# A hand-written order of 634 pieces of a fused retention and channel-mix kernel: its last 264 pieces in another order

## The chip, the cores and the metric

The kernel runs on one core of a Trainium2 chip. The metric is the device time of one execution in microseconds (us), taken on the chip; smaller is better. One further execution was recorded by the hardware profiler; the views of the profile come from that one.

## What is computed

The first half is a recurrent retention layer: 4 batches, 8 heads, 768 tokens, head width 64, with a decay `gamma` for each head. The second half is a channel mix on its output of width 512: two mixes of each token with the token before, a square-of-relu layer of width 1024, and a sigmoid gate.

```
state = gamma * state + k_t (outer) v_t           # for each head
y_t   = q_t . state / 8
x     = y, heads side by side                     # 4 x 768 x 512
xk    = mu_k * x + (1 - mu_k) * x_prev;  xr the same with mu_r
k     = relu(xk @ w_k);  v = (k * k) @ w_v
out   = sigmoid(xr @ w_r) * v
```

All inputs and the output are float32.

## The kernel before, in words

The 3072 tokens are cut into 12 blocks of 256 (n = 0 to 11, three to a batch). Everything is written out in one string, ORDER, as about 634 pieces. A piece is a code, the block, sometimes more numbers, the PSUM banks that it writes after an @, and the engine after a ~ (v VectorE/DVE, a ScalarE/ACT, p GpSimd/POOL, s SyncE/SP; no letter is TensorE/PE). The loop at the end of the kernel walks the string once and emits the instructions of each piece, so **the string is the program order of every engine's queue**; semaphores between the engines follow from the data. No other planner acts on it at run time. Each engine takes its own pieces strictly in the order of the string, and waits where a piece's data or buffer isn't ready.

The pieces that matter here, with the line of the instruction as the profile gives it:

- `lq`, `lk`, `lv` (L229, L234): loads of q, k, v of a block. `Tq`, `Tk` (L271, L277): transposes on PE, 32 small matmuls each for blocks 6 to 11; `Eq`, `Ek` (L240, ACT) copy them out of PSUM.
- `S` (L317, 32 matmuls) scores, `M` (L346, DVE) their mask; `vs` (L252, DVE) scales v; `C` (L365) the new state, `U` (L418, DVE) adds the old one in four steps, `G` decays it (L427 as one DVE instruction, L423 as four ACT instructions). `I` (L440) and `Y` (L461 and L440) make the retention's output in PSUM, `D` (L506, DVE, two instructions) scales it into x.
- `dx` (L528, DVE) is x minus x_prev; `X` (L557, DVE) mixes it, w = 0 for xk and w = 1 for xr, in four slices j. Blocks 3 and 4, 6 and 7, 9 and 10 share these.
- `K` (L571 for shared blocks, four matmuls of 512 columns; L581 for single ones, eight of 256): xk @ w_k. `Qa` (L590, ACT) relu, `Qb` (L598, L602, ACT) square. `R` (L611, four of 512): the gate's matmul; `s` (L617, ACT) its sigmoid.
- `V` (L623): (k*k) @ w_v for half a block of tokens, in two halves of four matmuls of 512 columns; `O` (L629, DVE) multiplies with the gate and frees the PSUM bank; `st` (L636, SP) stores 256 KB. For the last half block `Vc` (L641, eight of 256 columns), `Oc` (L648) and `sc` (L656) do this in two column halves.
- `z` are matmuls on zeros at the start, `cm` (L678, DVE) makes the masks, `mt` and `me` turn the mu vectors.

Two kinds of buffers tie the queues together. PSUM has eight banks: a PE piece that begins a bank waits until the last reader of that bank (an ACT or DVE piece) is through. And rings in SBUF: the output tiles OS are a ring of four, numbered 2n + tb, so `O.8.1` (17) writes the tile that `st.6.1` (13) has to have stored, and the gate tiles RS are a ring of four as well.

PE alternates between full matmuls (128 x 128 weights: K, R, V, Vc) and small ones (64 x 64 tiles: T, S, C, I, Y). A stretch of small pieces in a row is called a small run below.

Of the kernel before, what the change touches and what calls it, by code (L numbers as in the profile page):

```python
# [29 lines left out]
S.1.1@23 M.1.1~v C.1@01 U.1.0~v z.2@4 I.1@23 S.1.0@67 X.0.0.1~v t.0.1.2~a X.0.0.2~v Tk.2@0 t.0.1.3~a  # L30
t.0.0.0~a M.1.0~v X.0.0.0~v z.2@4 Y.1 t.0.1.1~a X.0.0.3~v Ek.2~a K.0.0@0 K.0.1@6 lq.4~p U.1.1~v
G.1~a wr~p lk.4~p D.1~v dx.1~v X.1.0.2~v X.1.0.0~v K.0.2@1 Qa.0.0~a Qb.0.0~a Qa.0.2~a lq.3~p
X.1.0.1~v X.1.0.3~v X.1.1.0~v Qa.0.1~a K.0.3@0 Qa.0.3~a lk.3~p vs.2~v Tq.2@1 X.1.1.2~v K.1.3@6
K.1.0@0 C.2@7 U.2.0~v lv.3~p Eq.2~a S.2.1@23 M.2.1~v S.2.0@45 M.2.0~v Qb.0.3~a lv.4~p K.1.1@1
X.1.1.1~v Qa.1.0~a t.0.1.0~a K.1.2@7 I.2@23 Qb.0.1~a Qa.1.1~a wv.0~p Qb.0.2~a Tq.4@01 Eq.4~a Y.2
Qa.1.3~a Qb.1.1~a X.0.1.3~v X.1.1.3~v R.1.1@4 Tk.4@01 Ek.4~a J.2 R.1.0@6 Qa.1.2~a s.1.0~a X.0.1.2~v
X.0.1.1~v X.0.1.0~v R.0.1@5 s.0.1~a s.1.1~a R.0.0@7 s.0.0~a S.4.1@01 Qb.1.0~a D.2~v dx.2~v X.2.0.2~v
X.2.0.0~v S.4.0@23 Tq.3@4 Eq.3~a X.2.0.1~v wv.1~p X.2.0.3~v Tk.3@7 lq.5~p Ek.3~a K.2.2@5 Qa.2.2~a
K.2.3@4 M.4.1~v M.4.0~v Qa.2.3~a Qb.2.3~a lk.6~p S.3.1@67 M.3.1~v S.3.0@01 vs.3~p C.3@23 U.3.0~a
Qb.2.2~a K.2.1@4 Qa.2.1~a K.2.0@2 Qa.2.0~a I.3@45 lq.6~p vs.4~v C.4@67 U.3.1~v X.2.1.1~v V.0.1.0@3  # L40
M.3.0~v V.1.0.0@2 G.3~a U.4.0~v I.4@01 X.2.1.3~v U.4.1~v J.3 Qb.1.3~a Y.4 Qb.2.0~a lk.5~p X.2.1.2~v
X.2.1.0~v Y.3 D.3~v dx.3~v V.0.0.0@7 V.0.1.1 O.0.1~v Tq.5@45 J.4 D.4~v dx.4~v R.2.0@6 Qb.2.1~a
V.0.0.1 O.0.0~v X.3.0.1~v Eq.5~a Qb.1.2~a V.1.0.1 X.3.0.2~v O.1.0~v Tq.6@01 Eq.6~a Tk.6@45 Ek.6~a
st.0.0~s lk.7~p st.1.0~s V.1.1.0@3 V.1.1.1 O.1.1~v s.2.0~a R.2.1@0 s.2.1~a lv.5~p X.3.0.0~v
X.3.0.3~v Tk.7@67 Ek.7~a G.4~a S.6@45 M.6~v Tk.5@23 Ek.5~a vs.5~v V.2.0.0@0 K.3.2@1 Qa.3.2~a K.3.0@6
S.5.0@23 M.5.0~v S.5.1@45 C.5@1 U.5.0~v K.3.3@7 Qb.3.2~a Qa.3.0~a lq.7~p K.3.7@6 Qa.3.3~a Qa.3.7~a
lv.6~p lq.8~p vs.6~v M.5.1~v V.2.0.1 st.0.1~s I.5@67 O.2.0~v st.2.0~s C.6@23 U.6.0~a U.6.1~v U.6.2~v
K.3.6@1 Qa.3.6~a lk.9~p X.3.1.3~v Y.5 Tq.7@45 Eq.7~a U.6.3~v X.3.1.2~v I.6@01 J.5 X.3.1.0~v D.5~v
X.3.1.1~v Qb.3.3~a G.6~a V.2.1.0@2 K.3.1@3 V.2.1.1 O.2.1~v Qb.3.7~a Qa.3.1~a Qb.3.1~a dx.5~v K.3.4@4
K.3.5@5 Qa.3.5~a X.5.0.0~v X.5.0.3~v R.3.1@2 s.3.1~a lv.7~p Qa.3.4~a X.5.0.1~v Qb.3.4~a R.3.0@5  # L50
R.4.0@2 s.3.0~a s.4.0~a Qb.3.0~a X.5.0.2~v vs.7~v K.5.2@4 S.7@67 st.1.1~s M.7~v Qb.3.5~a Y.6
Qb.3.6~a lv.10~p C.7@23 U.7.0~v X.5.1.1~v Qa.5.2~a K.5.0@5 R.4.1@6 Qa.5.0~a D.6~v s.4.1~a V.4.0.0@4
# [745 lines left out]
```

## Time and profile before

| what | value |
|---|---|
| median of 3 runs (lowest to highest) | 154.2 us (153.81 to 154.3) |
| the profiled execution's own time | 154.38 us |
| its span, first to last instruction | 152.6 us |
| granted clock | 1.0 |
| busy: PE / DVE / ACT / POOL | 144.1 / 128.7 / 100.6 / 55.3 us |
| moved by DMA | 22.16 MB |

The profiled execution's own time has 1.8 us outside the span. "Busy" counts a matmul from its start to its modelled end, so that neighbours overlap; PE at 94% of the span says that it hardly stopped, not that each matmul was as short as it could be. The chain of waits follows the work back from the last instruction and puts each stretch of time down to one engine and line, or to "issue", when an engine stood still and the profile shows nothing that it waited for. DMA rows tell the time from an issue to the landing.

### The profile page before, as it was taken

The numbers are of one execution on the slowest core, as the hardware profiler recorded it, in microseconds if no ns is written. First come the engines' busy times: TensorE is split into PE (matmuls) and PEld (weight loads), VectorE is DVE, ScalarE is ACT, GpSimd is POOL, SyncE is SP. The second block draws the span as 40 slices with busy tenths as digits, with TensorE's granted clock in tenths as the row PEclk, the third lists the DMA queues.
The fourth block names the chain that finished last, engine by engine and source line by source line (L and its number), as shares of the span: only waits on it lengthen the run. The fifth ranks groups of instructions, "written<-read, shape, count | busy, mean of one in ns | idle before, by whom it ended". The sixth has DMA issues, their size and how long they took to land.

```text
span 152.6 us, 5532 instructions
## 1 busy us (share of the span) xinstructions
PE 144.1 (94%) x2426; PEld 82.9 (54%) x2426; DVE 128.7 (84%) x214; ACT 100.6 (66%) x187; POOL 55.3 (36%) x65
## 2 busy tenths in 40 slices
...
GB/s 137 215 224 200 207 229 194 170 249 210 196 167 207 236 250 112 290 275 203 206 191 225 83 0 136 81 73 0 4 4 75 0 205 1 14 54 4 158 117 206
DMA packets 45624, 22.16 MB, mean 145 GB/s; under 512 B 37400, under 2 KB 41248, under 8 KB 45600
## 3 DMA queue, kind: packets, MB, share of 16 engines
...
q8 instruction: 19, 0.31, 0.8%
q10 hardware_dynamic: 304, 0.18, 0.5%
q14 instruction: 5, 0.04, 0.1%
...
## 4 chain that ended last, share of the span: by engine, by line
PE 91%; DVE 3%; ACT 2%; issue 1%; DVEq 0%
PE ps L623 27%; PE ps L581 14%; PE ps L611 14%; PE ps L571 14%; PE ps L701 4%; PE ps L277 3%; PE ps L440 2%; PE ps L271 2%; DVE a L353 2%; PE ps L330 1%; PE ps L477 1%; ACT qT L240 1%; PE ps L317 1%; PE ps L461 1%; PE ps L641 1%; PE ps L365 1%
## 5 line engine op out<-in xcount | busy, mean ns | idle before, releaser
L623 PE MATMUL ps<-wv,k2s 128*128 128x512 f16 x184 | 43.3, 380 | 0.0
L590 ACT ACTIVATE kr<-ps 128x512 f32<-128x512 f32 x48 | 27.4, 596 | 21.5 <-PE ps L581 11.1
L623 PEld LDWEIGHTS <-k2s 128*128 128x128 f16 x184 | 17.0, 98 | 19.3 <-ACT k2s L602 0.2
L629 DVE SCALAR_TENSOR_TENSOR os<-ps,rs 128x512 f32<-128x512 f32 x23 | 15.5, 685 | 12.4 <-ACT rs L617 7.1
L611 PE MATMUL ps<-wr,xr 128*128 128x512 f16 x96 | 23.5, 379 | 0.0
L581 PE MATMUL ps<-xk,wk 128*128 128x256 f16 x192 | 23.4, 273 | 0.0
L571 PE MATMUL ps<-xk,wk 128*128 128x512 f16 x96 | 22.9, 379 | 0.0
L229 POOL DMA_DIRECT2D k<-in_k_dram x20 | 17.9, 908 | 11.1 <-PE ps L383 6.8
L581 PEld LDWEIGHTS <-wk 128*128 128x128 f16 x192 | 18.3, 98 | 4.4 <-issue 0.2
L240 ACT COPY qT<-ps 128x1024 f16<-128x1024 f16 (+1 forms) x13 | 12.4, 951 | 9.2 <-PE ps L277 7.8
L557 DVE SCALAR_TENSOR_TENSOR xr<-dx,mu,xT 128x256 f16<-128x256 f32 (+1 forms) x32 | 18.0, 579 | 0.1
L617 ACT ACTIVATE rs<-ps 128x512 f32<-128x512 f32 x24 | 13.7, 594 | 6.1 <-DVE os L629 3.2
L229 POOL DMA_DIRECT2D v<-in_v_dram x18 | 16.0, 904 | 3.6 <-DMA wr<-in_moe_w_r_dram 1.9
L557 DVE SCALAR_TENSOR_TENSOR xk<-dx,mu,xT 128x256 f16<-128x256 f32 (+1 forms) x32 | 17.1, 581 | 0.2
L353 DVE TENSOR_TENSOR a<-ps,c_sb 128x1024 f16<-128x1024 f32 (+1 forms) x14 | 14.6, 1066 | 0.7 <-PE ps L338 0.4
L602 ACT ACTIVATE k2s<-kr 128x512 f16<-128x512 f32 x24 | 14.6, 626 | 0.2
L571 PEld LDWEIGHTS <-wk 128*128 128x128 f16 x96 | 9.1, 98 | 10.3
L611 PEld LDWEIGHTS <-xr 128*128 128x128 f16 x96 | 9.1, 98 | 10.2 <-DVE xr L557 0.3
L598 ACT ACTIVATE k2s<-kr 128x512 f16<-128x512 f32 x24 | 14.4, 625 | 0.3
L240 ACT COPY kT<-ps 128x1024 f16<-128x1024 f16 (+1 forms) x13 | 12.3, 944 | 2.9 <-PE ps L271 2.0
L528 DVE TENSOR_TENSOR dx<-xT 128x1024 f32<-128x1024 f32 x11 | 13.5, 1223 | 0.3
L252 DVE TENSOR_TENSOR vs<-v,csm_sb 128x1024 f16<-128x1024 f32 x10 | 12.2, 1219 | 0.2 <-DMA v<-in_v_dram 0.2
...
## 6 DMA issues: line engine op xcount, KB each, us to landing
out_dram<-os SPq DMA_DIRECT2D x23, 256.0 KB, 3.0
v<-in_v_dram POOLq DMA_DIRECT2D x18, 256.0 KB, 7.3
q<-in_q_dram POOLq DMA_DIRECT2D x11, 256.0 KB, 7.8
k<-in_k_dram POOLq DMA_DIRECT2D x21, 128.0 KB, 8.9
...
wk<-in_moe_w_k_dram POOLq DMA_DIRECT2D x2, 512.0 KB, 11.2
...
```

What stands on the lines that cost most here:

```text
L229: e.dma_start(out=dst[:, :, i * D : i * D + D], in_=src[:, i * P : i * P + P].rearrange("h p d -> p h d"),)
L240: e.copy(out=out, in_=in_)
L353: nc.vector.tensor_tensor(out=a_full(n)[:, i, :, j0:j1], in0=pairs(banks("S", n, i, j0))[:, :, j0:j1], in1=(below if wide(n) else causal[: ...
L557: nc.vector.scalar_tensor_tensor(out=XM[w](k)[:, j, t0:t1], in0=DX(k)[:, j, t0:t1], scalar=mu[:, w * NCO + j : w * NCO + j + 1], in1=x[:, ...
L571: nc.tensor.matmul(banks("K", n, g), lhsT=wk16[:, co, g * P : g * P + P], rhs=XM[0](k)[:, co, :], start=(co == 0), stop=(co == NCO - 1),)
L581: nc.tensor.matmul(pz[:, i, :], lhsT=wk16[:, co, fo * P : fo * P + P], rhs=XM[0](k)[:, co, m * TM + t0 : m * TM + t1], start=(i == 0 and c ...
L590: nc.scalar.activation(out=kr, in_=banks("K", n, g, *u), func=AF.Relu)
L598: nc.scalar.activation(out=k2s[:, n % 3 : n % 3 + 2, g, :], in_=kr, func=AF.Square,)
L602: nc.scalar.activation(out=K2(n)[:, w * g : w * g + w, t0:t1], in_=kr.rearrange("p a t -> p (a t)").rearrange("p (i t) -> p i t", i=w), fu ...
L611: nc.tensor.matmul(banks("R", n, tb), lhsT=XM[1](k)[:, co, t : t + P], rhs=wr16[:, co, :], start=(co == 0), stop=(co == NCO - 1),)
L623: nc.tensor.matmul(banks("V", n, tb), lhsT=K2(n)[:, fo, tb * P : tb * P + P], rhs=wv16[:, fo, :], start=(fo == 0), stop=(fo == NFO - 1),)
L629: nc.vector.scalar_tensor_tensor(out=OS(2 * n + tb), in0=banks("V", n, tb), scalar=1.0 / (KSC * KSC), in1=RS(2 * n + tb), op0=ALU.mult, op ...
```

## The change

Three things are edited. First, the mask piece `cm` is split into three pieces that stand one after another in the same place, on the same engine, with the same instructions. Second, at the start the banks of `Tk.0.2.4` and `Tq.0.2.4` are swapped (2 and 3), and with them that of the `z.2` behind. Third, from `dx.7 X.6.0.2 V.4.1.0` on, the rest of the string (264 pieces) has another order and other PSUM banks; the pieces themselves are the same, but `G.9` and `G.10` go from DVE to ACT. Up to there the order is the same.

The old lines come first and then the new ones; the lines left out differ only in where they break.

```diff
-cm gy.0~v mu~a lv.0~p lq.0.0.2~s lk.0.0.2~s ck.0.0.2~a cq.0.0.2~a z.12@6 Tq.0.0.2@0 Tk.0.0.2@1 gy.1~v
-z.1@2 mt@2 Ek.0.0.2~a Eq.0.0.2~a S.0.1.0.2@01 S.0.0.0.2@45 me~a lk.0.2.4~p Tk.0.2.4@2 Ek.0.2.4~a
-lq.0.2.4~p vs.0~v C.0@67 U.0.0~v Tq.0.2.4@3 Eq.0.2.4~a lq.1~p lk.1~p M.0.1.0.2~v z.2@2 S.0.1.2.4@23
...
-O.3.1~v st.2.1~s st.3.1~s Y.7 dx.6~v D.7~v Tq.10@23 V.3.0.1 Eq.10~a G.7~a dx.7~v X.6.0.2~v V.4.1.0@5
-V.4.1.1 X.6.0.0~v R.5.0@0 R.5.1@1 K.5.3@2 Qa.5.3~a Qb.5.3~a O.3.0~v s.5.0~a K.5.1@4 X.6.0.1~v lq.9~p
-lk.10~p Qa.5.1~a Qb.5.1~a lv.11~s s.5.1~a X.6.0.3~v K.6.3@2 Qa.6.3~a K.6.2@3 K.6.5@4 Qa.6.2~a
-U.8.0~v Qa.6.5~a X.6.1.2~v V.5.0.0@0 st.3.0~s X.6.1.0~v K.6.4@1 Qa.6.4~a O.4.1~v U.8.1~v X.6.1.1~v
-U.8.2~v I.8@45 S.8@67 Tk.10@23 Ek.10~a V.5.0.1 lv.9~p X.6.1.3~v vs.9~v K.6.6@1 Qb.6.2~a M.8~v
-Qa.6.6~a Qb.6.5~a S.10@67 O.5.0~v Y.8 M.10~v D.8~v vs.10~v dx.8~v st.5.0~s st.4.0~s Tk.9@23 Ek.9~a
-V.5.1.0@1 V.5.1.1 X.8.1.3~v vs.11~v O.5.1~v lk.11~p Qb.6.3~a Tk.11@23 Qb.6.4~a X.8.0.1~v X.8.0.3~v
-lq.11~p Tq.11@67 Ek.11~a X.8.1.2~v Tq.9@45 Eq.9~a K.6.1@0 Qa.6.1~a Eq.11~a R.6.0@2 s.6.0~a K.6.7@4
-R.6.1@5 s.6.1~a Qa.6.7~a C.9@23 S.11@67 X.8.0.0~v C.10@01 K.6.0@5 U.9.0~a Qa.6.0~a Qb.6.0~a U.9.1~v
-X.8.0.2~v Qb.6.6~a U.9.2~v U.9.3~v G.9~v Qb.6.1~a R.7.0@4 s.7.0~a K.8.1@5 Qa.8.1~a K.8.0@3 Qa.8.0~a
-R.7.1@2 s.7.1~a K.8.2@4 Qa.8.2~a V.6.0.0@3 U.10.0~v X.8.1.1~v U.10.1~v U.10.2~v st.4.1~s U.10.3~v
-M.11~v G.10~v I.9@45 Qb.6.7~a C.11@67 S.9@01 M.9~v Qb.8.0~a V.6.0.1 V.7.1.0@2 V.7.1.1 U.11.0~v
-U.11.1~v I.10@01 U.11.2~v I.11@67 O.6.0~v Y.9 D.9~v dx.9~v V.6.1.0@3 V.6.1.1 O.6.1~v K.8.3@4
-Qa.8.3~a Qb.8.2~a Y.10 D.10~v dx.10~v X.9.0.3~v X.9.0.1~v X.9.0.0~v Y.11 X.9.0.2~v D.11~v st.5.1~s
-st.6.1~s V.7.0.0@3 Qb.8.1~a V.8.0.0@4 V.8.1.0@5 Qb.8.3~a V.8.0.1 V.7.0.1 O.7.0~v O.7.1~v X.8.1.0~v
-dx.11~v X.11.0.2~v V.8.1.1 K.9.4@0 K.9.6@1 K.9.5@6 Qa.9.5~a Qb.9.5~a K.9.1@3 K.9.7@2 Qa.9.7~a
-Qb.9.7~a X.11.0.3~v X.11.1.0~v X.11.0.0~v R.8.0@6 K.9.0@2 s.8.0~a Qa.9.6~a Qa.9.0~a Qb.9.0~a K.9.2@7
-K.9.3@1 Qa.9.2~a X.11.1.3~v X.11.0.1~v X.9.1.0~v K.11.0@2 Qa.11.0~a Qb.11.0~a R.8.1@7 Qb.9.2~a
-s.8.1~a st.7.0~s st.6.0~s Qb.9.6~a O.8.0~v X.9.1.1~v K.11.3@2 K.11.1@4 X.9.1.2~v Qa.11.3~a X.9.1.3~v
-R.10.1@7 K.11.2@6 R.9.1@2 Qa.9.3~a Qa.11.1~a O.8.1~v R.9.0@1 Qa.9.1~a Qb.9.1~a Qb.9.3~a V.9.1.0@3
-Qb.11.1~a X.11.1.1~v X.11.1.2~v Qa.11.2~a V.10.0.0@4 V.10.1.0@6 Qa.9.4~a Qb.9.4~a V.10.1.1 R.11.0@0
-s.9.0~a V.9.1.1 st.7.1~s V.9.0.0@1 V.9.0.1 st.8.1~s Qb.11.2~a V.10.0.1 s.9.1~a V.11.0.0@2 s.10.1~a
-O.10.1~v O.9.1~v st.9.1~s R.10.0@3 O.9.0~v Qb.11.3~a st.9.0~s R.11.1@1 s.11.0~a V.11.0.1 st.10.1~s
-Vc.11.1.1@0 O.11.0~v s.10.0~a st.8.0~s O.10.0~v s.11.1~a Oc.11.1.1~v Vc.11.1.0@1 st.10.0~s st.11.0~s
-Oc.11.1.0~v sc.11.1.0~s sc.11.1.1~a
+cm.0~v cm.1~v cm.2~v gy.0~v mu~a lv.0~p lq.0.0.2~s lk.0.0.2~s ck.0.0.2~a cq.0.0.2~a z.12@6
+Tq.0.0.2@0 Tk.0.0.2@1 gy.1~v z.1@2 mt@2 Ek.0.0.2~a Eq.0.0.2~a S.0.1.0.2@01 S.0.0.0.2@45 me~a
+lk.0.2.4~p Tk.0.2.4@3 Ek.0.2.4~a lq.0.2.4~p vs.0~v C.0@67 U.0.0~v Tq.0.2.4@2 Eq.0.2.4~a lq.1~p
+lk.1~p M.0.1.0.2~v z.2@3 S.0.1.2.4@23 U.0.1~v lv.1~p lk.2~p I.0@01 S.0.0.2.4@67 M.0.0.2.4~v wk.0~p
...
+Ek.8~a V.3.1.1 V.3.0.0@4 C.8@67 O.3.1~v st.2.1~s st.3.1~s Y.7 dx.6~v D.7~v Tq.10@23 V.3.0.1 Eq.10~a
+G.7~a dx.7~v X.6.0.2~v V.4.1.0@5 R.5.1@2 s.5.1~a K.5.3@0 Qa.5.3~a R.5.0@2 U.8.0~v O.3.0~v V.4.1.1
+lv.9~p lk.10~p lq.9~p Tk.10@01 s.5.0~a U.8.1~v X.6.0.1~v Ek.10~a X.6.0.0~v Tk.9@23 Ek.9~a K.5.1@7
+Qa.5.1~a X.6.0.3~v K.6.0@4 lq.11~p Qb.5.1~a Qa.6.0~a U.8.2~v I.8@01 vs.9~v S.8@23 M.8~v O.4.1~v
+st.4.1~s K.6.4@7 Qa.6.4~a vs.10~v X.6.1.2~v K.6.2@6 C.9@23 Qa.6.2~a Qb.6.2~a U.9.0~a Y.8 U.9.1~v
+D.8~v U.9.2~v U.9.3~v X.6.1.3~v Qb.5.3~a Tq.9@45 V.5.1.0@6 V.5.1.1 O.5.1~v Eq.9~a lk.11~p K.6.3@7
+Qa.6.3~a K.6.7@4 Qa.6.7~a V.5.0.0@7 C.10@45 Qb.6.0~a X.6.1.0~v S.9@23 M.9~v G.9~a Qb.6.3~a Tq.11@01
+Eq.11~a V.5.0.1 dx.8~v X.6.1.1~v st.4.0~s K.6.1@6 Qb.6.7~a Qa.6.1~a Qb.6.1~a X.8.0.3~v X.8.0.0~v
+U.10.0~v U.10.1~v K.6.5@2 Qa.6.5~a st.3.0~s lv.11~s K.6.6@0 Qa.6.6~a Qb.6.6~a R.6.0@6 s.6.0~a
+O.5.0~v U.10.2~v U.10.3~v R.7.0@2 s.7.0~a R.6.1@7 s.6.1~a I.9@45 X.8.0.2~v S.10@23 Tk.11@01 Ek.11~a
+X.8.0.1~v K.8.1@7 Qb.6.5~a Qa.8.1~a Qb.8.1~a vs.11~v st.5.1~s K.8.0@6 C.11@01 M.10~v Qb.6.4~a
+X.8.1.0~v X.8.1.2~v Y.9 D.9~v G.10~a U.11.0~v st.5.0~s U.11.1~v U.11.2~v Qa.8.0~a I.10@23 V.6.1.0@7
+V.6.1.1 O.6.1~v V.6.0.0@4 V.6.0.1 I.11@01 S.11@67 M.11~v dx.9~v V.7.1.0@5 V.7.1.1 Y.10 D.10~v
+dx.10~v X.9.0.3~v X.9.0.0~v Y.11 Qb.8.0~a X.9.0.2~v R.7.1@6 s.7.1~a X.9.0.1~v V.7.0.0@7 V.7.0.1
+K.8.3@6 O.7.0~v X.9.1.0~v D.11~v X.8.1.1~v Qa.8.3~a Qb.8.3~a K.8.2@2 Qa.8.2~a Qb.8.2~a X.8.1.3~v
+dx.11~v X.11.1.0~v X.11.1.1~v X.9.1.1~v V.8.1.0@6 K.9.2@3 X.11.0.0~v K.9.6@7 Qa.9.6~a V.8.1.1
+Qa.9.2~a Qb.9.2~a X.11.0.3~v K.9.5@7 K.9.3@3 K.9.0@2 Qa.9.0~a Qb.9.6~a V.8.0.0@0 V.8.0.1 Qb.9.0~a
+Qa.9.5~a Qb.9.5~a Qa.9.3~a O.7.1~v st.7.1~s X.9.1.2~v X.11.0.1~v O.6.0~v K.9.7@1 R.8.1@7 s.8.1~a
+K.9.1@5 R.8.0@7 X.9.1.3~v X.11.0.2~v st.6.1~s O.8.1~v R.9.1@4 R.9.0@6 K.11.0@3 K.11.3@2 s.8.0~a
+Qa.9.1~a Qb.9.1~a Qb.9.3~a V.10.0.0@5 V.9.0.0@7 Qa.11.0~a Qb.11.0~a Qa.11.3~a s.9.0~a K.9.4@6
+R.10.0@2 Qa.9.7~a X.11.1.3~v st.6.0~s K.11.1@1 Qa.11.1~a Qa.9.4~a K.11.2@3 Qb.9.7~a Qb.9.4~a
+Qa.11.2~a X.11.1.2~v O.8.0~v st.7.0~s st.8.1~s st.8.0~s V.9.1.0@1 V.10.1.0@6 s.10.0~a V.9.1.1
+V.10.0.1 s.9.1~a O.9.1~v st.9.1~s Qb.11.2~a Qb.11.3~a O.10.0~v st.10.0~s R.10.1@4 V.9.0.1 s.10.1~a
+O.9.0~v R.11.1@4 V.10.1.1 Qb.11.1~a V.11.0.0@7 R.11.0@5 s.11.0~a st.9.0~s Vc.11.1.1@1 s.11.1~a
+O.10.1~v st.10.1~s Oc.11.1.1~v V.11.0.1 O.11.0~v st.11.0~s sc.11.1.1~a Vc.11.1.0@4 Oc.11.1.0~v
+sc.11.1.0~s
```

The code for `cm`, the only code that is edited:

```diff
         for m in (1 << l for l in range(7)):
             nc.vector.tensor_scalar_add(out=count[:, m : 2 * m], in0=count[:, 0:m], scalar1=float(m))
 
-    def masks(e):
+    def masks(e, part):
         for out, col, op in (
-            (ident, 0, ALU.is_equal), (causal[:, 0], 1, ALU.is_ge), (causal[:, 1], 1, ALU.is_gt),
-            (step, 2, ALU.is_ge), (below, 0, ALU.is_ge),
-        ):
-            nc.vector.tensor_scalar(
+            ((ident, 0, ALU.is_equal),),
+            ((causal[:, 0], 1, ALU.is_ge), (causal[:, 1], 1, ALU.is_gt)),
+            ((step, 2, ALU.is_ge), (below, 0, ALU.is_ge)),
+        )[part]:
+            e.tensor_scalar(
                 out=out, in0=count[:, 0 : out.shape[-1]], scalar1=mark[:, col : col + 1], scalar2=None, op0=op
             )
 
```

More of the change, by code (lines that the diff above doesn't have):

```diff
@@ L24 @@
 ORDER = """
-cm gy.0~v mu~a lv.0~p lq.0.0.2~s lk.0.0.2~s ck.0.0.2~a cq.0.0.2~a z.12@6 Tq.0.0.2@0 Tk.0.0.2@1 gy.1~v
-z.1@2 mt@2 Ek.0.0.2~a Eq.0.0.2~a S.0.1.0.2@01 S.0.0.0.2@45 me~a lk.0.2.4~p Tk.0.2.4@2 Ek.0.2.4~a
-lq.0.2.4~p vs.0~v C.0@67 U.0.0~v Tq.0.2.4@3 Eq.0.2.4~a lq.1~p lk.1~p M.0.1.0.2~v z.2@2 S.0.1.2.4@23
-U.0.1~v lv.1~p lk.2~p I.0@01 S.0.0.2.4@67 M.0.0.2.4~v wk.0~p wk.1~p G.0~a z.2@6 Tq.1@6 Eq.1~a vs.1~p
-lq.2~p Tk.1@7 Ek.1~a M.0.0.0.2~v M.0.1.2.4~v Y.0 D.0~v t.0.0.3~a t.0.0.2~a t.0.0.1~a lv.2~p z.2@4
@@ L30 @@
[L30 to L52, printed above, removed]
@@ L53 @@
-V.4.0.1 V.3.1.0@5 U.7.1~v Qb.5.0~a X.5.1.3~v U.7.2~v I.7@01 X.5.1.2~v U.7.3~v Tq.8@67 Eq.8~a
-X.5.1.0~v O.4.0~v lv.8~p vs.8~v Qb.5.2~a lq.10~p lk.8~p Tk.8@23 Ek.8~a V.3.1.1 V.3.0.0@4 C.8@67
-O.3.1~v st.2.1~s st.3.1~s Y.7 dx.6~v D.7~v Tq.10@23 V.3.0.1 Eq.10~a G.7~a dx.7~v X.6.0.2~v V.4.1.0@5
-V.4.1.1 X.6.0.0~v R.5.0@0 R.5.1@1 K.5.3@2 Qa.5.3~a Qb.5.3~a O.3.0~v s.5.0~a K.5.1@4 X.6.0.1~v lq.9~p
-lk.10~p Qa.5.1~a Qb.5.1~a lv.11~s s.5.1~a X.6.0.3~v K.6.3@2 Qa.6.3~a K.6.2@3 K.6.5@4 Qa.6.2~a
-U.8.0~v Qa.6.5~a X.6.1.2~v V.5.0.0@0 st.3.0~s X.6.1.0~v K.6.4@1 Qa.6.4~a O.4.1~v U.8.1~v X.6.1.1~v
@@ new lines @@
+lk.0.2.4~p Tk.0.2.4@3 Ek.0.2.4~a lq.0.2.4~p vs.0~v C.0@67 U.0.0~v Tq.0.2.4@2 Eq.0.2.4~a lq.1~p
+lk.1~p M.0.1.0.2~v z.2@3 S.0.1.2.4@23 U.0.1~v lv.1~p lk.2~p I.0@01 S.0.0.2.4@67 M.0.0.2.4~v wk.0~p
+wk.1~p G.0~a z.2@6 Tq.1@6 Eq.1~a vs.1~p lq.2~p Tk.1@7 Ek.1~a M.0.0.0.2~v M.0.1.2.4~v Y.0 D.0~v
+t.0.0.3~a t.0.0.2~a t.0.0.1~a lv.2~p z.2@4 S.1.1@23 M.1.1~v C.1@01 U.1.0~v z.2@4 I.1@23 S.1.0@67
+X.0.0.1~v t.0.1.2~a X.0.0.2~v Tk.2@0 t.0.1.3~a t.0.0.0~a M.1.0~v X.0.0.0~v z.2@4 Y.1 t.0.1.1~a
+X.0.0.3~v Ek.2~a K.0.0@0 K.0.1@6 lq.4~p U.1.1~v G.1~a wr~p lk.4~p D.1~v dx.1~v X.1.0.2~v X.1.0.0~v
@@ new lines @@
+K.0.2@1 Qa.0.0~a Qb.0.0~a Qa.0.2~a lq.3~p X.1.0.1~v X.1.0.3~v X.1.1.0~v Qa.0.1~a K.0.3@0 Qa.0.3~a
+lk.3~p vs.2~v Tq.2@1 X.1.1.2~v K.1.3@6 K.1.0@0 C.2@7 U.2.0~v lv.3~p Eq.2~a S.2.1@23 M.2.1~v S.2.0@45
+M.2.0~v Qb.0.3~a lv.4~p K.1.1@1 X.1.1.1~v Qa.1.0~a t.0.1.0~a K.1.2@7 I.2@23 Qb.0.1~a Qa.1.1~a wv.0~p
+Qb.0.2~a Tq.4@01 Eq.4~a Y.2 Qa.1.3~a Qb.1.1~a X.0.1.3~v X.1.1.3~v R.1.1@4 Tk.4@01 Ek.4~a J.2 R.1.0@6
+Qa.1.2~a s.1.0~a X.0.1.2~v X.0.1.1~v X.0.1.0~v R.0.1@5 s.0.1~a s.1.1~a R.0.0@7 s.0.0~a S.4.1@01
@@ new lines @@
+Qb.1.0~a D.2~v dx.2~v X.2.0.2~v X.2.0.0~v S.4.0@23 Tq.3@4 Eq.3~a X.2.0.1~v wv.1~p X.2.0.3~v Tk.3@7
+lq.5~p Ek.3~a K.2.2@5 Qa.2.2~a K.2.3@4 M.4.1~v M.4.0~v Qa.2.3~a Qb.2.3~a lk.6~p S.3.1@67 M.3.1~v
+S.3.0@01 vs.3~p C.3@23 U.3.0~a Qb.2.2~a K.2.1@4 Qa.2.1~a K.2.0@2 Qa.2.0~a I.3@45 lq.6~p vs.4~v
+C.4@67 U.3.1~v X.2.1.1~v V.0.1.0@3 M.3.0~v V.1.0.0@2 G.3~a U.4.0~v I.4@01 X.2.1.3~v U.4.1~v J.3
+Qb.1.3~a Y.4 Qb.2.0~a lk.5~p X.2.1.2~v X.2.1.0~v Y.3 D.3~v dx.3~v V.0.0.0@7 V.0.1.1 O.0.1~v Tq.5@45
+J.4 D.4~v dx.4~v R.2.0@6 Qb.2.1~a V.0.0.1 O.0.0~v X.3.0.1~v Eq.5~a Qb.1.2~a V.1.0.1 X.3.0.2~v
@@ new lines @@
+O.1.0~v Tq.6@01 Eq.6~a Tk.6@45 Ek.6~a st.0.0~s lk.7~p st.1.0~s V.1.1.0@3 V.1.1.1 O.1.1~v s.2.0~a
+R.2.1@0 s.2.1~a lv.5~p X.3.0.0~v X.3.0.3~v Tk.7@67 Ek.7~a G.4~a S.6@45 M.6~v Tk.5@23 Ek.5~a vs.5~v
+V.2.0.0@0 K.3.2@1 Qa.3.2~a K.3.0@6 S.5.0@23 M.5.0~v S.5.1@45 C.5@1 U.5.0~v K.3.3@7 Qb.3.2~a Qa.3.0~a
+lq.7~p K.3.7@6 Qa.3.3~a Qa.3.7~a lv.6~p lq.8~p vs.6~v M.5.1~v V.2.0.1 st.0.1~s I.5@67 O.2.0~v
+st.2.0~s C.6@23 U.6.0~a U.6.1~v U.6.2~v K.3.6@1 Qa.3.6~a lk.9~p X.3.1.3~v Y.5 Tq.7@45 Eq.7~a U.6.3~v
+X.3.1.2~v I.6@01 J.5 X.3.1.0~v D.5~v X.3.1.1~v Qb.3.3~a G.6~a V.2.1.0@2 K.3.1@3 V.2.1.1 O.2.1~v
```

5 lines of the change are left out of this document (added).

## Prediction

> **What bounds the kernel now.** I read the page first: busy times and the chain that ended last.
>
> ```profile
> PE 144.1 (94%) x2426; PEld 82.9 (54%) x2426; DVE 128.7 (84%) x214; ACT 100.6 (66%) x187; POOL 55.3 (36%) x65
> ...
> q8 instruction: 19, 0.31, 0.8%
> ...
> PE 91%; DVE 3%; ACT 2%; issue 1%; DVEq 0%
> ```
>
> PE carries 91% of the chain through the span of 152.6 us, so the time is PE's work, PE's pauses, and what follows PE's last matmul. The work is the same in both orders. The edit can move only the rest, so I looked for that in the chain in order of time, from 80 us on (the last common piece of PE ends there).
>
> ```profile
> 92.43 0.38 PE ps L317 x32
> ...
> 95.35 0.31 PE ps L277 x24
> 95.67 0.45 issue
> 96.11 0.80 PE ps L277 x72
> ...
> 114.59 0.38 PE ps L461 x32
> 114.96 0.15 PE ps L440 x14
> 115.11 0.28 PE ps L461 x31
> 115.39 0.17 PE ps L440 x10
> 115.57 5.29 PE ps L623 x24
> ...
> 139.88 4.32 PE ps L623 x20
> ...
> 146.79 1.76 PE ps L641 x16
> ```
>
> A stream of full matmuls runs at 4.32/20 = 0.216 us each, of half width at 1.76/16 = 0.110 us. Entering a small run costs 0.38 - 0.28 = 0.10 us and leaving it 5.29 - 24 x 0.216 = 0.11 us. With these prices the chain from 80 to 148.5 us closes but for one pause, 0.45 us at 95.67 us in the middle of Tk.11, put down to "issue": no data, no bank. What is it? The page has 19 packets on the instruction queue q8, 0.31 MB, and 2426 + 2426 PE instructions: 16 KB and some 255 of them to a packet. DMA of 93 to 95 us (40 slices of 0.05 us), of 138 to 141 us (slices of 0.075 us), and the counts of records up to the pause and up to the last packet:
>
> ```profile
> DMA  0000000009000075997969799798999969989999
> q8 instruction: 1, 0.02, 3.8%
> ```
>
> ```profile
> DMA  0000000000000000000008000000000000000000
> q8 instruction: 1, 0.02, 2.0%
> ```
>
> ```profile
> 0.00:95.67 95.67, 91.66 (x1758) 53.82 (x1759) 90.36 (x151) 70.14 (x132) 55.27 (x65) 1.00 1.32 192
> 0.00:139.58 139.58, 135.12 (x2378) 78.23 (x2379) 124.57 (x207) 98.29 (x184) 55.27 (x65) 1.00 0.94 146
> ```
>
> A packet starts at 93.45 us, two microseconds ahead of the pause. Before the pause PE took 32 + 48 + 32 + 8 + 24 = 144 matmuls, 288 instructions, in the 3.24 us from 92.43. I read it so: the next block of code was asked for when the one before it was entered, near 92.4 us, and became usable at 96.1, about 3.7 us later, while PE ate a block in 3.2. The pause is at 3517 records, and a later boundary should be 5 x 256 on, at 4797; the last packet starts at record 4757, 40 instructions before PE gets there. So in a stretch of full matmuls, where eight instructions take 0.86 us, the sequencer is about 40 ahead, some 4 us, and the fetch is early. It is late only where two small runs follow each other too closely.
>
> **The change, part by part.**
>
> *Code transfers.* Laying the new order out with the prices above and counting on in steps of 256, boundaries fall at 84.6 (start of Tk.10), 89.5 (C.9), 94.5 (V.5.0.0), 102.1 (I.9), 105.1 (Y.9), 111.8 (Y.10), 119.8 and 144 us. The shortest block is I.9 to Y.9: 3.0 us, even denser than the one that stalls now. But seven full pieces, 56 instructions in 6 us, stand ahead of I.9, so its boundary is passed by the sequencer near 98 us and the next block is there by about 102, against a need at 105. All other blocks have 4.9 us or more, against 3.7. I take the whole pause as gone: **-0.45 us**. Bounds: -0.45, and +0.3 (the pause is kept and, as 3.0 us is less than 3.2, grows by 0.3).
>
> The Trainium skill, page "Runtime: NRT & Kernel Launch", section "Instruction fetch mechanics", speaks against this term: the sequencer fetches the next 16 KB block while it runs the current one, and crossing a boundary is "mostly hidden". By that rule this term would be 0, and the sum below -0.19; the 0.45 us here fits it only if "mostly" leaves room for dense runs, and no run so far shows which.
>
> *Small runs.* From V.4.1.0 on the old order has seven (I.8 S.8 Tk.10; S.10 Y.8 Tk.9; Tk.11 Tq.11 Tq.9; C.9 S.11 C.10; I.9 C.11 S.9; I.10 I.11 Y.9; Y.10 Y.11), the new one eight (Tk.10 Tk.9; I.8 S.8; C.9 Y.8 Tq.9; C.10 S.9 Tq.11; I.9 S.10 Tk.11; C.11 Y.9 I.10; I.11 S.11; Y.10 Y.11). One more: 0.10 + 0.11 = **+0.2 us**. Bounds 0.1 and 0.3.
>
> *New waits of PE.* For each PE piece I added up the queue of the engine that feeds it or empties its bank. Most end 0.1 to 0.4 us ahead. Banks taken again after one piece (K.9.6 and K.9.5 on 7, R.8.1 and R.8.0 on 7, R.10.1 and R.11.1 on 4) leave 0.02 to 0.04 us, no tighter than K.9.7 and K.9.0 on 2 in the old order, which shows no pause. The one place with nothing to spare is R.9.0 on bank 6: V.8.1 wrote that bank, O.8.1 empties it, and O.8.1 writes the OS tile of st.6.1. SP reaches st.6.1 only behind st.7.1, which waits for O.7.1. Durations for DVE, the stores in threes, and a store alone:
>
> ```profile
> 106.05 1.21 DVE L346 TENSOR_TENSOR a<-ps,c_sb 128x1024 f16<-128x1024 f32 x1
> ...
> 114.66 0.68 DVE L629 SCALAR_TENSOR_TENSOR os<-ps,rs 128x512 f32<-128x512 f32 x1
> 115.26 1.48 DVE L506 TENSOR_TENSOR xT<-ps,gy_sb 128x512 f32<-128x512 f32 x2
> 116.78 1.23 DVE L528 TENSOR_TENSOR dx<-xT 128x1024 f32<-128x1024 f32 x1
> 118.04 2.74 DVE L557 SCALAR_TENSOR_TENSOR xk<-dx,mu,xT 128x512 f16<-128x512 f32 x4
> ...
> 125.25 0.88 DVE L557 SCALAR_TENSOR_TENSOR xk<-dx,mu,xT 128x256 f16<-128x256 f32 x2
> ```
>
> ```profile
> out_dram<-os SPq DMA_DIRECT2D x3, 256.0 KB, 2.4
> ```
>
> ```profile
> out_dram<-os SPq DMA_DIRECT2D x1, 256.0 KB, 2.0
> ```
>
> DVE from S.11's end to O.7.1: about 0.2 until its last result is there, M.11 1.13 + dx.9 1.14 + D.10 1.52 + dx.10 1.26 + four X.9 2.64 + O.7.0 0.6 + X.9.1.0 0.66 + D.11 1.4 + two X.8 0.9 + dx.11 1.3 + X.11 twice 0.8 + X.9.1.1 0.66 + X.11 twice 0.8 = 15.0. Then O.7.1 0.7, 0.4 for the issue of st.7.1, 2.4 until st.6.1 lands, O.8.1 0.7: 19.2 us. PE in that time: 76 full matmuls 16.4, 16 half ones 1.76, Y.10 and Y.11 0.98 (114.59 to 115.57), leaving the run before 0.11: 19.2 us. Nothing is left, so **+0.1 us**; bounds 0 and +0.6 (a landing of 3.0, the page's median).
>
> *The end.* Old: when PE ends at 146.79 + 1.76 = 148.55, st.10.0 and st.11.0 have just been issued and the two halves of the last tile follow; DMA is full and the last half lands 2.6 us after its issue at 149.11.
>
> ```profile
> 148.20 0.81 SPq L636 DMA_DIRECT2D out_dram<-os  x2
> 149.11 0.40 SPq L656 DMA_DIRECT2D out_dram<-os  x1
> ```
>
> ```profile
> out_dram<-os SPq DMA_DIRECT2D x2, 256.0 KB, 2.8
> out_dram<-os ACTq DMA_DIRECT2D x1, 128.0 KB, 2.1
> out_dram<-os SPq DMA_DIRECT2D x1, 128.0 KB, 2.6
> ```
>
> New: V.11.0.1 stands between Vc.11.1.1 and Vc.11.1.0, so the first half is stored 0.9 us earlier, st.10.0 and st.10.1 go some 7 and 4 us before the end, and only st.11.0 (O.11.0 ends 0.2 us before PE) is ahead of the last half. 256 KB less queue in front of it; it should land like a store alone, 2.0 to 2.1 us: **-0.5 us**. Bounds 0 (it still takes 2.6) and -0.9. Oc.11.1.0 now stands behind sc.11.1.1's issue, but writes the other half of the tile.
>
> *Parts that I cost at nothing.* The masks: same instructions, engine and place. The swapped banks: mt's last reader ends before either transpose begins, and z.2 waits for the same copy Ek.0.2.4. G.9 and G.10 on ACT: four short instructions, 1.1 us each, for 0.42 us of DVE; U.10.0 and U.11.0 come more than a microsecond later; without that cover they would cost DVE up to 1 us. Loads: POOL's order changes by a place or two and Tk.10 goes from 90.3 to 84.5 us; lk.10's last half is issued near 70 and lands within 9.
>
> ```profile
> k<-in_k_dram POOLq DMA_DIRECT2D x21, 128.0 KB, 8.9
> ```
>
> ```profile
> 69.53 0.88 POOL L229 DMA_DIRECT2D k<-in_k_dram  x1 [1.06 <-PE ps L611]
> ```
>
> That leaves about 5 us. lv.11 goes behind three stores on SP, from 79 to about 91 us; vs.11 stands at 102, and SP's stores behind it wait for later results anyway.
>
> *Sum.* -0.45 + 0.2 + 0.1 - 0.5 = -0.65 us on the profiled execution: span 152.6 to 151.95, own time 154.38 to 153.7. That execution is 0.18 us above the median; on the median 154.2 the same sum gives **153.6 us** (-0.4%).
>
> **The rivals.**
>
> - *The pause comes back* (the I.9 to Y.9 block at about 105 us, or it was no code transfer). For it: 3.0 us is the densest block of all, and the packet of 93.45 ended well before 96.1. Against: the early packet at 139.6. Without the 0.45 us the sum is -0.2: 154.0. The skill page above, taken strictly, gives this case too.
> - *A store wait takes its place* at R.9.0: landing 3.0, +0.6 for +0.1: 154.1. For it the page's median; against it 2.4 in a group of three late in the kernel, with no loads around.
> - *The end gains nothing*: the last half still lands after 2.6 us because st.11.0 is ahead of it: 154.1. Against: one store of 256 KB ahead in place of two and a half.
> - *Slower*: the same tile of O.8.1, with a landing as in the loaded stretch, where the slowest store took 6.4 us.
>
> ```profile
> DMA to landing us min/median/max: 2.0/3.0/6.4
> ```
>
>   PE would stand 6.4 - 2.4 = 4.0 us at R.9.0: 157.5. It decides from a landing of about 3.6 us, which adds 1.1 us to the forecast and ends 0.3% above before. Against: by 126 us all loads are through.
>
> **How the numbers follow.** A measurement of this kernel can tell about 0.3%, 0.46 us, from no change. Forecast 0.60 (153.2 to 153.9, nearly all of it faster by over 0.3%), the pause comes back 0.13, store wait 0.09, the end 0.09, slower 0.09. Faster by over 0.3%: 0.57; within: 0.33; slower: 0.10. The range runs from the good ends of the bounds (small runs 0.1, no wait, -0.9 at the end: 153.0) to the cases at 154.0 to 154.1 with a second small one added: 153.0 to 154.6.
>
> **What would show it.** Right: no "issue" pause on PE after 80 us, PE's last matmul at about 148.4, the last store landing about 2.0 us after its issue. Wrong: an issue pause near 105 us; R.9.0 (L611 near 129 us) waiting for DVE os; a last landing of 2.6; or PE waiting for ACT at one of the banks with 0.02 us to spare, which would make the prediction too low by the sum of such waits.

## The result and the profile after

The new order takes **153.38 us**, the median of 22 executions, against 154.25 us for the kernel before, also of 22. The ratio of the two is 0.9949, with a 95% interval of 0.9931 to 0.9968. That is -0.79 us (-0.5 to -1.1), so the kernel is faster by more than 0.3%. The forecast was 153.6. Executions in a slower state (one of the new kernel's, 159.87 us) count in the medians and not in the ratios.

The profiled execution of the new kernel took 153.06 us itself and its span is 151.3 us, against 154.38 and 152.6. This pair differs by 1.3 us, more than the medians do, because the execution profiled before lay 0.13 above its median and the one after lies 0.32 below. I therefore read from the pair where time moved, and take the amounts from the ratios.

The lines of the edited code are one further down in the new kernel (L277 is now L278, L611 is L612, L623 is L624, L641 is L642). The page of the new kernel, busy times, instruction queue and chain:

```profile
PE 143.5 (95%) x2426; PEld 82.9 (55%) x2426; DVE 127.5 (84%) x212; ACT 103.4 (68%) x195; POOL 55.3 (37%) x65
...
q8 instruction: 19, 0.31, 0.8%
...
PE 86%; ACT 3%; DVE 3%; POOL 2%; DMA 2%; issue 1%; SPq 0%; DVEq 0%
```

PE's share of the chain, 86% in place of 91%, is no part of the change: a second profiled execution of the new kernel has 92%. PE has the same 2426 matmuls and the same 19 packets of code. ACT has eight instructions more and DVE two fewer: `G.9` and `G.10`, one DVE instruction or four ACT ones each.

The chain of the new kernel in order of time (start, length, what), from the piece that also stands last in the common part:

```profile
79.19 1.83 PE ps L624 x8
...
94.93 0.38 PE ps L366 x32
95.31 0.27 PE ps L318 x32
95.58 0.27 PE ps L278 x32
95.84 0.97 PE ps L624 x4
...
99.40 2.59 PE ps L612 x12
...
102.49 0.28 PE ps L278 x32
...
127.20 2.70 PE ps L612 x12
...
147.22 0.89 PE ps L642 x8
148.10 0.02 issue
148.13 0.42 DVE os L649
```

Three things are to be read here. No "issue" piece of PE stands between 79 us and PE's last matmul: the transposes of `Tq.11` (L278 at 95.58) and of `Tk.11` (102.49) run through in 0.27 and 0.28 us for 32, where the chain before has 24, a pause of 0.45, and 72. The twelve matmuls of L612 that hold `R.9.0` (127.20) take 2.70 us; elsewhere in this chain (99.40) twelve of this shape take 2.59, so PE stood 0.1 us. And PE ends at 147.22 + 0.89 = 148.11; the forecast had about 148.4.

The issues of stores in the new kernel, the last 7 us, with the median time from issue to landing, and then SP's last issue in the chain of waits:

```profile
out_dram<-os SPq DMA_DIRECT2D x2, 256.0 KB, 2.0
out_dram<-os ACTq DMA_DIRECT2D x1, 128.0 KB, 1.7
out_dram<-os SPq DMA_DIRECT2D x1, 128.0 KB, 1.8
```

```profile
148.58 0.33 SPq L657 DMA_DIRECT2D out_dram<-os  x1
```

These rows answer to 2.8, 2.1 and 2.6 before. The last half is issued 0.47 us after PE's end (before 149.11 - 148.55 = 0.56) and lands 1.8 us later instead of 2.6.

So the pair divides as follows. Up to the last common piece the new execution is 0.11 us ahead (79.30 against 79.19), in code that is practically the same: scatter. From there to PE's end it took 68.92 us against 69.25: -0.33. From PE's end to the end of the span it took 3.2 against 4.05: -0.85.

### The profile page after: what moved, and what is told of

Its sections match the earlier page's. It is cut to its first block, busy times and chain, and to the rows that moved or that the text cites. A ratio compares the mean times of both kernels' runs of the same rounds, so it can differ in the third digit from the quotient of the medians.

```text
span 151.3 us, 5540 instructions
## 1 busy us (share of the span) xinstructions
PE 143.5 (95%) x2426; PEld 82.9 (55%) x2426; DVE 127.5 (84%) x212; ACT 103.4 (68%) x195; POOL 55.3 (37%) x65
## 4 chain that ended last, share of the span: by engine, by line
PE 86%; ACT 3%; DVE 3%; POOL 2%; DMA 2%; issue 1%; SPq 0%; DVEq 0%
PE ps L624 27%; PE ps L612 14%; PE ps L572 14%; PE ps L582 13%; PE ps L278 3%; PE ps L441 2%; DMA k2s<-in_k_dram 2%; PE ps L272 2%; DVE a L354 2%; PE ps L478 1%; ACT qT L241 1%; POOL vs L253 1%; PE ps L366 1%; PE ps L462 1%; PE ps L642 1%; POOL k L230 1%
## 5 line engine op out<-in xcount | busy, mean ns | idle before, releaser
L624 PE MATMUL ps<-wv,k2s 128*128 128x512 f16 x184 | 44.1, 380 | 0.0
L624 PEld LDWEIGHTS <-k2s 128*128 128x128 f16 x184 | 17.1, 98 | 18.9 <-ACT k2s L603 0.4
L612 PE MATMUL ps<-wr,xr 128*128 128x512 f16 x96 | 23.5, 379 | 0.0
L612 PEld LDWEIGHTS <-xr 128*128 128x128 f16 x96 | 9.1, 98 | 10.7 <-issue 0.5
```

What stands on the lines that cost most here:

```text
L612: nc.tensor.matmul(banks("R", n, tb), lhsT=XM[1](k)[:, co, t : t + P], rhs=wr16[:, co, :], start=(co == 0), stop=(co == NCO - 1),)
L624: nc.tensor.matmul(banks("V", n, tb), lhsT=K2(n)[:, fo, tb * P : tb * P + P], rhs=wv16[:, fo, :], start=(fo == 0), stop=(fo == NFO - 1),)
```

## The experiments

Theory: most of the gain is the end (a last store with less in front of it), a smaller part is the pause for code, and an additional small run and a short wait at `R.9.0` take some of it back. Rivals: the head of the string does something; the pause is no transfer of code; the gain comes out of the middle. Each ratio is to the kernel before in the same batch of runs, whose median was 154.17 to 154.52 us.

| run | median us | ratio to before (95%) | in us |
|---|---|---|---|
| new kernel | 153.38 | 0.9949 (0.9931 to 0.9968) | -0.79 |
| new kernel again | 153.42 | 0.9956 (0.9935 to 0.9977) | -0.68 |
| only the head new | 153.99 | 0.9990 (0.9973 to 1.0006) | -0.15 |
| old order, end rearranged | 153.41 | 0.9952 (0.9930 to 0.9975) | -0.74 |
| old order, gap in the small runs | 154.21 | 0.9980 (0.9962 to 0.9998) | -0.31 |
| old order, both of these | 153.03 | 0.9935 (0.9912 to 0.9959) | -1.00 |
| new order, end as of old | 154.01 | 0.9983 (0.9957 to 1.0010) | -0.26 |
| new order, st.6.1 earlier | 153.23 | 0.9939 (0.9905 to 0.9973) | -0.94 |
| new order, st.6.1 later | 155.08 | 1.0052 (1.0026 to 1.0079) | +0.80 |
| new order, G.9 and G.10 on DVE | 153.84 | 0.9980 (0.9965 to 0.9995) | -0.31 |
| new order, 640 transposes behind | 167.45 | one execution | |

The last column is (ratio - 1) x 154.25.

### The head alone

The split mask and the swapped banks, with the old order behind them.

```diff
-cm ... Tk.0.2.4@2 ... Tq.0.2.4@3 ... z.2@2
+cm.0~v cm.1~v cm.2~v ... Tk.0.2.4@3 ... Tq.0.2.4@2 ... z.2@3
```

> The old order with the new start alone (masks in three pieces, banks 2 and 3 swapped for the transposes of heads 4 to 7 of block 0). Theory (the gain is in the tail: the code-transfer pause and the last stores): no change, ratio 1.000 within 0.002, the pause of about 0.45 us near 95.7 us still there, the last store landing 2.6 us after its issue. Rival (the start gives the 0.1 us that separates the two traces at 79 us, or more): 0.999 or less.

Its interval holds 1. Its chain, at the place of the pause, and its last store:

```profile
95.13 0.31 PE ps L277 x24
95.44 0.36 issue
95.80 0.80 PE ps L277 x72
```

```profile
out_dram<-os SPq DMA_DIRECT2D x1, 128.0 KB, 2.6
```

The landing is as before, and the pause nearly so. The ratio alone, 0.9990, doesn't part the two theories, and its interval reaches down to -0.4 us. The traces help: `Tq.10`, before which the orders differ in the head alone, ends at 79.2 to 80.2 us in four profiled executions with the old head, and at 78.9 to 81.2 us in seven with the new one. The head does nothing that can be measured in this scatter.

### The old order with only its end rearranged

```diff
-... V.11.0.1 st.10.1~s Vc.11.1.1@0 O.11.0~v s.10.0~a st.8.0~s O.10.0~v s.11.1~a Oc.11.1.1~v
-Vc.11.1.0@1 st.10.0~s st.11.0~s Oc.11.1.0~v sc.11.1.0~s sc.11.1.1~a
+... Vc.11.1.1@5 s.11.1~a Oc.11.1.1~v V.11.0.1 O.11.0~v st.11.0~s sc.11.1.1~a
+Vc.11.1.0@7 Oc.11.1.0~v sc.11.1.0~s
```

`st.8.0`, `st.10.1`, `s.10.0`, `O.10.0` and `st.10.0` go ahead of this stretch.

> The old order with the end alone put as in the new one: stores of blocks 8 and 10 issued earlier, the first half of the last tile ahead of V.11.0.1, banks 5 and 7 for the two halves. Theory (one store of 256 KB less in front of the last half): the last store lands 1.8 to 2.1 us after its issue in place of 2.6, time between PE's last matmul and the end 3.2 us in place of 4.05, ratio about 0.995 (0.993 to 0.997), the pause near 95.7 us unchanged. Rival (the end of PE's work sets the time and the landing is fixed): 1.000.

Nine moved pieces bring -0.74 us, nearly all of what the reorder of 264 brings. Which of the nine matter was not tried. Chain and last store of this kernel:

```profile
95.54 0.31 PE ps L277 x24
95.85 0.06 issue
95.91 0.80 PE ps L277 x72
...
147.46 0.89 PE ps L641 x8
148.35 0.02 issue
148.37 0.42 DVE os L648
```

```profile
out_dram<-os SPq DMA_DIRECT2D x1, 128.0 KB, 1.8
```

The landing goes from 2.6 to 1.8 us. The pause is there again, in the same place and with the same instructions ahead of it, but, other than expected, only 0.06 us long. In three executions with practically identical code up to that place (the kernel before, the head alone, this one) it was 0.45, 0.36 and 0.06 us. Each time the packet of code starts (93.45, 93.15, 93.55 us) 2.4 to 2.7 us before PE goes on (96.11, 95.80, 95.91).

### The old order with a gap in the small runs

```diff
-... Tk.11@23 ... Tq.11@67 Ek.11~a X.8.1.2~v Tq.9@45 Eq.9~a K.6.1@0 Qa.6.1~a Eq.11~a ...
+... K.6.1@0 Tk.11@23 ... Tq.11@67 Qa.6.1~a Ek.11~a X.8.1.2~v Tq.9@45 K.6.0@0 Eq.9~a Qa.6.0~a Eq.11~a ...
```

`K.6.1` now stands between the small run of `Tk.9` and that of `Tk.11`, and `K.6.0` behind the second; their `Qa` go with them, and `S.11` and `Qa.6.7` move by a place.

> The old order with one full piece, K.6.1, put between the two small runs around the pause (and K.6.0 behind them, the ACT pieces moved with them), so that the 256 instructions take 0.9 us longer. The same code paused for 0.45, 0.36 and 0.06 us in three profiled executions so far, each time with 0.2 us more in restarting. Theory (the pause is a block of code that is usable 3.3 to 3.7 us after the run is entered): no pause, Tk.11, Tq.11 and Tq.9 take 0.9 us in place of 1.2 to 1.6, ratio 0.996 to 0.999. Rival (the pause belongs to these transposes, not to the code): the pause stays beside the same piece, ratio 1.000 or a little above.

```profile
94.36 1.83 PE ps L623 x8
96.19 0.86 PE ps L571 x4
97.06 0.93 PE ps L277 x96
97.99 0.97 PE ps L571 x4
...
103.55 1.90 PE ps L581 x16
```

The 96 transposes run through in 0.93 us; before they took 0.31 + 0.80 = 1.11 and the pause beside it, so starting again costs 0.18 us more. One piece of 0.86 us in front removes both. The whole edit is worth -0.31 us, with an interval that just leaves out zero. That is not the pause alone. From 94.36 us (`V.5.1.0`) to PE's end at 149.02 it takes 54.66 us, against 55.03 before (93.52 to 148.55): 0.37 less, although pause and restart were 0.63, so the moved pieces cost about 0.26 us in short waits elsewhere. One of them can be seen at `K.8.1` and `K.8.0`, 1.90 us in place of 1.79 before.

### The new order with 640 small transposes behind its end

These are extra matmuls whose result nobody reads; they are there only to let PE eat code as fast as it can.

```diff
-sc.11.1.0~s
+sc.11.1.0~s sm.640@23
```

> The new order with 640 small transposes added behind everything, which nobody reads: 1280 PE instructions, five blocks of code, with almost no other transfers about. Theory (a block is asked for when the one before is entered and takes about 3.5 us): PE stands every 256 instructions, each block takes about 3.5 us, 15 to 18 us in all, with a packet of the instruction queue per block. Rival (code keeps pace with small matmuls): 640 x 0.0085 = 5.4 us without a pause.

PE's timeline from the first of these matmuls on (the idle time ahead in brackets), some stretches (length, PE and weight loads with their counts, and third from the end the granted clock), and DMA from 152 to 164 us, where 40 slices are 0.3 us each:

```profile
148.24 2.08 PE L663 MATMUL ps<-c_sb,q 64*64 64x64 f16 x228
152.55 1.24 PE L663 MATMUL ps<-c_sb,q 64*64 64x64 f16 x128 [2.24 <-issue]
156.01 1.92 PE L663 MATMUL ps<-c_sb,q 64*64 64x64 f16 x128 [2.22 <-issue]
159.74 1.92 PE L663 MATMUL ps<-c_sb,q 64*64 64x64 f16 x128 [1.81 <-issue]
163.46 0.59 PE L663 MATMUL ps<-c_sb,q 64*64 64x64 f16 x28 [1.81 <-issue]
```

```profile
0.00:150.40 150.40, 146.55 (x2654) 84.89 (x2655) 127.49 (x212) 103.26 (x195) 55.28 (x65) 1.00 0.91 147
...
152.50:153.80 1.30, 1.24 (x128) 1.13 (x128) 0.00 (x0) 0.00 (x0) 0.00 (x0) 0.96 0.05 13
156.00:157.90 1.90, 1.89 (x128) 1.78 (x128) 0.00 (x0) 0.00 (x0) 0.00 (x0) 0.50 0.03 9
```

```profile
DMA  0000020000000000020000000000020000000000
...
q8 instruction: 3, 0.05, 1.7%
```

PE stops after every 128 matmuls, that is 256 instructions, and a block starts each 3.46 to 3.73 us though its work is 1.24 to 1.92 us. The granted clock falls to 0.50 on the way, and there the same work takes 1.92 us; but the first stop, of 2.24 us, came at a clock of 1.00. DMA does nothing in these 12 us but carry one packet of code for each block: each starts in the slice about a microsecond after the block before was entered (153.5, 157.1, 160.7 us), and PE goes on 2.5 to 2.8 us after that slice's start. No data, no bank and no load from other transfers is left to explain the stops. The places fit too: the first stop comes after 2654 + 2655 = 5309 records, 7 x 256 after the 3517 at which the old kernel paused. The pauses of the old kernel are transfers of code. One thing more can be read in this run: the kernel's last half tile lands after 3.5 us, not 1.8. A packet of code starts at 150.1 us and takes 0.95 us, in the middle of that store, and the store's last kilobytes move from 151.1 to 151.8 us. That the packet held them up is likely, but was not tried.

### The new order with the end as of old

```diff
-... Vc.11.1.1@1 s.11.1~a O.10.1~v st.10.1~s Oc.11.1.1~v V.11.0.1 O.11.0~v st.11.0~s sc.11.1.1~a
-Vc.11.1.0@4 Oc.11.1.0~v sc.11.1.0~s
+... V.11.0.1 Vc.11.1.1@1 s.11.1~a O.11.0~v O.10.1~v Oc.11.1.1~v Vc.11.1.0@4 st.10.1~s st.11.0~s
+Oc.11.1.0~v sc.11.1.0~s sc.11.1.1~a
```

> The new order with the end put back to the old manner: V.11.0.1 ahead of Vc.11.1.1, O.10.1 behind O.11.0, st.10.1 and st.11.0 issued last, just ahead of the two halves. Theory (nearly all of the gain is at the end, since the pause, the eighth small run and R.9.0 cancel): the last half lands 2.6 us after its issue again, ratio to the old kernel 0.999 to 1.001, about 0.7 us slower than the new one. Rival (the tail's order gains on PE as well): 0.996 to 0.998.

```profile
out_dram<-os SPq DMA_DIRECT2D x1, 128.0 KB, 2.6
```

The landing is 2.6 us again, and the interval of the ratio holds 1. The ratio of 0.9983 lies between what the two theories expected, so that it decides for neither: without its end, the new order brings at most 0.7 us and perhaps nothing.

### st.6.1 earlier and later

`O.8.1` writes the tile that `st.6.1` stores, and `R.9.0` takes the bank that `O.8.1` frees. Once `st.6.1` goes ahead of `st.7.1`, once behind `st.6.0`.

```diff
-O.7.1~v st.7.1~s ... X.11.0.2~v st.6.1~s O.8.1~v ... X.11.1.3~v st.6.0~s
+O.7.1~v st.6.1~s st.7.1~s ... X.11.0.2~v O.8.1~v ... X.11.1.3~v st.6.0~s
```

```diff
-X.11.0.2~v st.6.1~s O.8.1~v ... X.11.1.3~v st.6.0~s
+X.11.0.2~v st.6.0~s st.6.1~s O.8.1~v ... X.11.1.3~v
```

> The new order with st.6.1 issued ahead of st.7.1. Theory (R.9.0 waits about 0.1 us for O.8.1, and O.8.1 for the landing of st.6.1): O.8.1 starts as soon as X.11.0.2 is through and the three R pieces take 2.6 in place of 2.7 us; ratio 0.994 to 0.995, hardly to be told from the new kernel's 0.9949. Rival (DVE's own queue makes O.8.1 late, the store had landed): O.8.1 starts at the same time, the 0.1 us stays.

> The new order with st.6.0 put ahead of st.6.1 on SP, so that st.6.1 waits for O.6.0 too. Theory (bank 6, O.8.1 and the store's landing hold R.9.0, as in the prediction's slower case): st.6.1 is issued near 127.4 in place of 125.9 us, lands near 129.9, PE stands 1.3 to 1.7 us at R.9.0, ratio 1.003 to 1.006: slower than the old kernel. Rival (O.8.1 is held by DVE's own queue or the tile isn't waited for): no pause at R.9.0, 0.995.

Earlier: the twelve matmuls with `R.9.0` take 2.59 us, so the 0.1 us is gone; the time cannot be told from that of the new kernel. The execution profiled here took 155.02 us, but what it lost lies before the common part's end: `Tq.10` ends at 81.19 us in place of 79.19, and from there to PE's end it takes 68.79 us in place of 68.92.

```profile
129.19 2.59 PE ps L612 x12
```

Later: what PE waits for after 80 us, and the chain there:

```profile
PE ps L612 <- DVE os L630: 1.6, 1, 1.6
```

```profile
126.67 0.33 SPq L637
...
127.06 2.33 DMA out_dram<-os
...
129.49 0.70 DVE os L630
...
130.23 1.02 PE ps L612 x4
```

One store ahead of another on SP and nothing else puts the landing of `st.6.1` at 129.4 us, DVE waits for it, and PE for DVE: 1.6 us by the trace, 155.08 - 153.42 = 1.66 us by the medians. This is the wait of the prediction's slower rival, brought about by a later issue in place of a longer landing: the store goes out 1.3 us later (127.06 against 125.72), and the delay goes into the time whole.

### G.9 and G.10 back on DVE

```diff
-G.9~a ... G.10~a
+G.9~v ... G.10~v
```

> The new order with G.9 and G.10 on DVE again, in the same places of the string. Theory (the move to ACT matters a little, since DVE has no slack there): the sums of the queues give two small waits of PE, 0.2 us at R.6.1 and 0.1 us at S.11, so about 0.3 us slower than the new kernel, ratio 0.996 to 0.998. Rival (the prediction's: it costs nothing either way, DVE is 0.8 us busier and ACT two microseconds freer): 0.995 as before.

It loses 0.42 us against the new kernel in the same batch (153.84 and 153.42); the intervals of the two ratios overlap, but from `Tq.10`'s end to PE's end its trace has 69.39 us, and that of the new kernel beside it 68.91. PE's timeline, first of this kernel, then of the new one, at `R.6.0` to `R.6.1` (twelve of R in one group) and at `S.11`:

```profile
99.61 3.01 PE L612 MATMUL ps<-wr,xr 128*128 128x512 f16 x12
...
109.77 0.68 PE L318 MATMUL ps<-qT,kT 64*64 64x64 f16 x32
```

```profile
99.24 2.75 PE L612 MATMUL ps<-wr,xr 128*128 128x512 f16 x12
...
109.14 0.44 PE L318 MATMUL ps<-qT,kT 64*64 64x64 f16 x32
```

PE stands 3.01 - 2.75 = 0.26 us ahead of `R.6.1`, whose bank `O.5.0` frees, and 0.68 - 0.44 = 0.24 at `S.11`, because DVE, with two more instructions of 0.42 us in its queue, is that much late. The waits are spread inside groups and too short for the table of waits, which shows none.

### The two small edits together, in the old order

The gap in the small runs and the rearranged end, with the rest of the old order.

> The old order with two small edits: one full piece between the two small runs, and the end as in the new order. Theory (pause and end are separate and add up): -0.3 and -0.7 us, ratio 0.993 (0.991 to 0.995), at least as fast as the new order, without an eighth small run. Rival (they overlap or the gap edit's gain was chance): 0.995 to 0.996.

153.03 us, -1.00 us: below both kernels by the median, though the interval overlaps that of the new order. The two edits alone gave -0.31 and -0.74, together -1.05: within the intervals they add up.

## Why the prediction was right

The direction, the size (-0.65 forecast, -0.79 measured) and the main cause were right. Step by step:

- **Code transfers (-0.45).** The mechanism is shown, by the gap and by the 640 transposes, and the new order has no pause. The size was that of one execution: the same code paused 0.45, 0.36 and 0.06 us, and each time 0.18 us more went into starting again, which the step left out. The gap edit, which removes both but costs some 0.26 us elsewhere, is worth -0.31 us by the ratio. The block of `I.9` to `Y.9`, the densest of the new order, did run through, as the step said, though with less to spare: its packet starts at 100.8 us, and by the 2.5 to 2.8 us above PE could go on at about 103.5 (an estimate), not 102, against a need at 105.
- **The rule of the Trainium skill.** The Trainium skill, page "Runtime: NRT & Kernel Launch", section "Instruction fetch mechanics", has the crossing of a block as mostly hidden. The runs disagree where one dense block follows another: with 1.24 to 1.92 us of work in a block, PE stood 1.8 to 2.2 us at each crossing. They agree where full matmuls stand ahead, as before `I.9`.
- **Small runs (+0.2) and `R.9.0` (+0.1).** The first has no run of its own, but its count and its price stand in the new chain: eight runs, 0.38 us in place of 0.27 for the 32 matmuls that begin one (94.93), 0.97 in place of 0.86 behind it (95.84). The second is: 2.70 against 2.59 us, gone when `st.6.1` goes earlier. The sum of 19.2 us against 19.2, put together from rows of the old trace, put the limit in the right place; that it came out to a tenth is more than some twenty rounded terms can promise.
- **The end (-0.5).** Right in kind, too small: a landing of 1.8 us instead of the 2.0 that I took from a whole store alone, though the last store is half of one, and the issue 0.09 us sooner: -0.85 us in the profiled pair. By the old order with the new end, it is -0.74 us.
- **Parts at nothing.** The head: nothing that could be measured. `G.9` and `G.10` on ACT: they cost nothing, but I priced only ACT's side. The rest of the new order needs the time that this gives DVE: without it the kernel is about 0.4 us slower.

The terms -0.31, -0.74, +0.2 and +0.1 add up to -0.75, close to the measured -0.79, but that is no test: the first two have an interval of some 0.3 us to either side, and the first contains the cost of the gap edit. The profiled executions, side by side, divide the gain better:

| profiled execution | pause in or at `Tk.11` | from `Tq.10`'s end to PE's end | from PE's end to the span's end |
|---|---|---|---|
| before | 0.45 | 69.25 | 4.1 |
| only the head new | 0.36 | 69.16 | 4.0 |
| old order, end rearranged | 0.06 | 68.86 | 3.2 |
| old order, gap in the small runs | none | 68.86 | 4.1 |
| old order, both of these | none | 68.89 | 3.2 |
| new kernel | none | 68.92 | 3.2 |
| new kernel again | none | 68.91 | 3.2 |
| new order, end as of old | none | 68.92 | 4.0 |

The end is worth 0.8 to 0.9 us in every one of them, and no other change moves it. On PE the new order is 0.2 to 0.3 us better than the two old executions with a long pause and no better than the one with 0.06 us. For the profiled pair the terms close: -0.45 - 0.18 + 0.21 + 0.11 = -0.31 on PE, against -0.33. So the mechanisms were right, but that the sum came out at the right size is partly luck: the end was taken about 0.3 us too small, and the pause from the longest of three. The slower rival did not come: with the store where the new order has it, the wait was 0.1 us. Its mechanism is real, as the later `st.6.1` shows.
